# Another order of weight slices in block 0, half of a cast on ScalarE, one product on VectorE

## The chip, the cores and the metric

One core of one Trainium2 chip runs the kernel. The metric is the device time of one execution in microseconds (us), the median of several runs. The engines are named as the profile names them: PE is TensorE (matmuls; PEld its weight loads), DVE is VectorE, ACT is ScalarE, POOL is GpSimd, and SP is SyncE, which here only issues DMAs. Each engine works through its own instruction queue in order; POOL issues DMAs in the same queue in which it computes.

## The reference

Linear attention over 8 batches (B), 8 heads, 576 tokens and 64 channels, then one expert layer with an ELU over all 4608 tokens:

```python
q_s = softmax(q, axis=-1)            # over the 64 channels
k_s = softmax(k, axis=2)             # over the 576 tokens
kv  = einsum('bhsd,bhse->bhde', k_s, v)
x   = einsum('bhsd,bhde->bhse', q_s, kv)   # -> [4608, 512]
h   = x @ w_in                       # w_in  [512, 2048]
g   = where(h > 0, h, exp(min(h, 0)) - 1)
out = g @ w_out                      # w_out [2048, 512]
```

The inputs and the output are float32.

## The kernel before

The expert layer runs in nine blocks: one for 512 tokens of each batch and a last one for the 64 tokens of each batch that are left over. A block has 16 steps, one for each 128-column slice of W1 (NCH is 16). Step s of block j does, in this order: the hidden matmuls of slice s (`hidden`: four on PE into one PSUM bank, then an exponential ES on ACT and, for most slices, a subtraction on POOL), the projection of an earlier slice (`project`: four matmuls with the slice's 128 rows of W2, LAG = 3 steps behind), and the ELU's last part on DVE (`elu`, which writes GT). PE's program order is thus hidden, project, hidden, project and so on, and PE reads GT of three steps before.

While block j runs, the engines prepare batch j + 1: softmax of q (`qmax`, `qsub`, `qexp`, `qsum`, `qmul`), of k (`kmax`, `ksub`, `kexp`), v cast to bf16 (`vconv`), the product kv, its scaling (`kfac`), the transposed q (`pturn`, copied out by `pwide`), and the attention (`att`, copied out by `xc`). Batch 0 is prepared ahead of block 0, by the string START; what is woven into block 0, for batch 1, is the table FIRST. An entry of FIRST has three strings of words for a step: the first is issued after `hidden`, the second after `project`, the third after `elu`. The order in these strings is the order in which each engine gets its instructions. A word may name the engine (`:dve`, `:act`, `:gp` for POOL).

Words that matter here:

- `w1:a:b` and `w2:a:b` issue, from POOL, one DMA for slices a to b-1 of W1 or W2 (256 KB a slice). `hidden` of slice c waits for W1's slice c, `project` for W2's.
- `load:V:1:RAB` issues from SP four DMAs of 288 KB, one for each pair of heads (slots 0 to 3), into VR; the word `hold` ahead of it makes SP wait for the latest hidden matmuls. Half A of a batch means slots 0 and 1, half B slots 2 and 3.
- `vconv:A` casts half A of v into VB and waits for slots 0 and 1; `kv:A` reads it. Words for part R of v and k (`vconv:R`, `ksub:R`, `kexp:R`) issue nothing for batch 1, and `kmax2:R` nothing at all: `vconv` (L566), `ksub_slot` (L447), `kexp_slots` (L490) and `kmax` (L341) return without an instruction for that part.
- `qmul:2` and `qmul:3` are q's last products for slots 2 and 3 of batch 0, read by `pturn:B` on PE. `xc:1:dve` copies the first attention product for block 0 on DVE.
- Bank 7 (AB) of PSUM is used in turn by `kspread`, `pturn:A`, `pturn0:R`, `rest0`, `pturn:B`, `kv:A` and the attention in block 0: PE writes it, ACT copies it out, and PE may write again only then.

Of the kernel before, what the change touches and what calls it, by code (L numbers as in the profile page):

```python
# [11 lines left out]
B, H, S, D = 8, 8, 576, 64  # L12
# [3 lines left out]
R = 4  # L16
# [19 lines left out]

AT = {"rawA": 0, "rawA2": 1, "rawB": 7, "rawB2": 4, "rawS": 3, "rawT": 2,
      "kturnA": 4, "kturnB": 5, "kvA": 6, "kvB": 4, "pturnA": 5, "pturnB": 5,  # L40
      "att0": 6, "att1": 2, "att2": 3, "att3": 4, "clip": (1, 2, 4, 6, 8, 10, 11, 17, 21, 30, 32, 33, 37, 42, 44)}
START = ("load:Q:0:1 load:K:0:0 load:K:0:1 warm:1:7 warm:4:7 qmax:1 warm:2:4 load:Q:0:3 qsub:1:dve "
# [3 lines left out]
         "w1:4:6 kacross:B kexp:S vconv:A:act kmin:A qsub:2:gp qsub:3:gp diag:act:B w2:2:3 qsum:0 kmin:B "  # L46
         "kexp:A load:V:0:3 kmin:T qexp:2 qmul:A:dve qsum:2 load:V:0:2 qexp:3 w1:6:9 "
         "qsum:3 vconv:B:gp load:K:1:M qmul:2:gp kexp:B kexp:T kv:A kfac:A:dve pturn:A kv:B "
         "pwide:A:act kfac:B:act warm:1:3 att:1 att:0 qmul:3:gp pturn:B xc:1:dve xc:0 h:2:4 "
         "pwide:B:act w2:3:4 att:2 att:3 xc:2 load:Q:1:A load:Q:1:R w2:4:6 h:0:2 xc:3 kmax2:AB ")  # L50
FIRST = {
    0: ("qmax:A ksub:R:dve", "", "qsub:0:dve"),
    1: ("w1:13:14", "w1:9:12", "qsub:1:dve"),
    2: ("", "qmax0:R", "w2:6:9"),
    3: ("hold qexp:A", "load:Q:1:B:act", ""),
    4: ("w1:12:13", "w2:9:13", "load:K:1:R qsum:A qsub0:R:dve"),
    5: ("w1:14:16", "kturn", "kacross vconv:R qmax:C"),
    6: ("", "qmul:A hold", "load:V:1:RAB"),
    7: ("qexp0:R", "", "diag qsub:2:dve"),
    8: ("qsub:D", "kspread load:K:2:MR copy ksub:1 qsum0:R", "qexp:C qmulr0:dve ksub:0 qsum:C"),  # L60
    9: ("pturn:A", "", "ksub:3 kexp:R qmul:B:dve pwide:A:act"),
    10: ("", "pturn0:R pwide0:R:act", "ksub:2:dve vconv:A:gp"),
    11: ("rest0 rcopy0:act", "kexp:A", ""),
    12: ("pturn:B w2:15:16", "pwide:B:act load:Q:2:ABR", "w2:13:15"),
    13: ("kv:A vconv:B:dve", "kfac:A:dve", "kexp:B peak2:B att:0 xc:0"),
# [55 lines left out]
class Gen:  # L121
# [760 lines left out]
    def hidden(self, j, c):  # L882
# [6 lines left out]
        for x, keys in self.pieces("ES", n, NE):  # L889
            mark = ["FINE"] if n < FINE else []  # L890
            if n in AT["clip"]:
                self.op("act", lambda: a.activation(ES[:, x], ps[:, x], AF.Relu, scale=-1.0), [f"bank{bank}"], keys + mark)  # L892
# [24 lines left out]
    def elu(self, j, c):  # L917
# [4 lines left out]
        for (x, eks), (_, keys) in zip(self.pieces("ES", n, NE), self.pieces("GT", n, NG)):  # L922
            how = (ES[:, x], -1.0, ps[:, x], ALU.add, ALU.max) if n in AT["clip"] else (
                ps[:, x], 0.0, ES[:, x], ALU.max, ALU.min)
# [173 lines left out]
    def first_batch(self):  # L1098

        at = AT  # L1100
        where = {"A": (at["rawA"], at["rawA2"]), "B": (at["rawB"], at["rawB2"]),
# [3 lines left out]
                   "qsum": self.qsum, "qmul": self.qmul}  # L1105
        for word in START.split():
            name, *args = word.split(":")
# [100 lines left out]
```

## Time and profile before

| | |
|---|---|
| device time, median of 3 runs | 309.68 us (309.59 to 310.59) |
| span of the profiled execution | 308.1 us |
| its instructions | 4839 |
| granted TensorE clock | 1.000 |
| HBM read, written | 38.27 MB, 9.45 MB |

The span goes from the first to the last instruction of the one execution that was profiled; it is what the profile tells of that execution's own time. A line of the timeline reads: start and duration in us, engine, line of the kernel, operation, tile written <- tiles read, shape, number of instructions merged, and in brackets how long the engine had been idle before it and what ended that. A line of the waits reads: who waited <- for whom, us in total, times, the longest. A line of DMA issues ends with the size and the us from issue to landing. A row by windows gives, for each engine, the busy us and the number of instructions, then the granted clock, the DMA's busy share and its GB/s. The rows below are of core 0, the only one.

### The profile page before, as it was taken

The page shows a single profiled execution, that of the slowest core. Times are in us where ns is not written, and L with a number is a line of the kernel's source. Part 1 is how long each engine was busy: PE and PEld are TensorE (multiplying, and loading weights), DVE is VectorE, ACT ScalarE, POOL GpSimd, SP SyncE. Part 2 cuts the span into 40 slices and gives each one's busy share as a digit, 9 for nine tenths or more (in the row PEclk, how much of TensorE's full clock was granted, in tenths as well). Part 3 has the DMA queues.
Part 4 walks back from the last instruction along what each step waited for, and adds up shares of the span by engine and source line. Part 5 has one row for each costly group of instructions (what it writes and reads, how often), then busy time and mean ns, then how long its engine had stood idle before and what let it go on. Part 6 is the DMA issues. An engine that isn't in the chain of part 4 may idle for free.

```text
span 308.1 us, 4839 instructions
## 1 busy us (share of the span) xinstructions
PE 297.6 (97%) x1733; PEld 240.1 (78%) x1733; DVE 235.0 (76%) x400; ACT 192.9 (63%) x358; POOL 171.3 (56%) x215
## 2 busy tenths in 40 slices
PE   7789899999999999999999999999999999999995
PEld 4467677788878888888888888888888888888884
DVE  6988978979959897999889988998895353335442
ACT  2678975577559784877587758775877543334432
POOL 2968873686436743786278637863686333333440
PEclk9999999999999999999999999999999999999999
DMA  7999999985708993768475846590512030003004
GB/s 261 393 340 364 372 345 257 273 253 145 191 3 246 261 251 105 223 122 231 133 217 144 208 143 209 146 198 3 172 23 57 2 136 0 0 2 136 0 0 136
DMA packets 60584, 51.63 MB, mean 168 GB/s; under 512 B 26897, under 2 KB 50705, under 8 KB 60561
## 3 DMA queue, kind: packets, MB, share of 16 engines
q1 hardware_dynamic: 52960, 41.23, 47.7%
q0 software_dynamic: 6400, 8.39, 10.5%
q10 hardware_dynamic: 1200, 1.72, 2.0%
q8 instruction: 13, 0.21, 0.3%
q14 instruction: 11, 0.08, 0.1%
HBM read 38.27 MB, written 9.45 MB: 155 GB/s over the span
## 4 chain that ended last, share of the span: by engine, by line
PE 85%; DMA 6%; POOL 4%; ACT 2%; DVE 2%; issue 1%
PE bank L933 40%; PE bank L912 40%; DMA W2S<-in_moe_w_out_dram 5%; PE bank L827 2%; POOL W1S L255 1%; PE bank L598 1%; DMA QR<-in_q_dram 1%; POOL QR L679 1%; POOL QS L708 1%; PE bank L805 1%; DVE KT L326 1%; DVE QF L672 0%; PE bank L560 0%; ACT ES L895 0%; ACT ES L893 0%
## 5 line engine op out<-in xcount | busy, mean ns | idle before, releaser
L933 PE MATMUL bank<-W2S,GT 128*128 128x512 f32 x572 | 153.4, 391 | 1.4 <-DMA W2S<-in_moe_w_out_dram 1.2
L896 POOL TENSOR_SCALAR ES<-ES 128x512 f32<-128x512 f32 (+1 forms) x130 | 85.8, 662 | 117.3 <-ACT ES L895 117.3
L912 PE MATMUL bank<-XT,W1S 128*128 128x512 f32 x512 | 138.4, 392 | 0.5 <-issue 0.3
L925 DVE SCALAR_TENSOR_TENSOR GT<-bank,ES 128x512 fp32r<-128x512 f32 (+1 forms) x130 | 87.9, 681 | 54.4 <-PE bank L912 40.6
L933 PEld LDWEIGHTS bank<-W2S,GT 128*128 128x128 f32 x572 | 106.3, 188 | 23.6 <-DMA W2S<-in_moe_w_out_dram 1.6
L895 ACT ACTIVATE ES<-bank 128x512 f32<-128x512 f32 (+1 forms) x130 | 76.0, 592 | 70.9 <-PE bank L912 70.7
L912 PEld LDWEIGHTS bank<-XT,W1S 128*128 128x128 f32 x512 | 94.1, 188 | 19.9 <-ACT XT L814 0.9
L679 POOL TENSOR_TENSOR QR<-QR,QM 128x512 f32<-128x512 f32 (+1 forms) x21 | 24.9, 1187 | 0.6 <-DVE QM L672 0.5
L684 ACT ACTIVATE QR<-QR 128x1024 f32<-128x1024 f32 (+3 forms) x19 | 19.0, 1006 | 3.1 <-DVE QR L679 3.1
L855 ACT ACTIVATE XT<-bank 128x320 fp32r<-128x320 f32 (+1 forms) x30 | 15.0, 501 | 9.4 <-PE bank L827 9.3
L689 DVE TENSOR_REDUCE QZ<-QR 128x16 f32<-128x1024 f32 (+1 forms) x14 | 18.8, 1343 | 0.6 <-ACT QR L684 0.6
L672 DVE TENSOR_REDUCE QM<-QR 128x16 f32<-128x1024 f32 (+1 forms) x14 | 18.8, 1342 | 0.0
L912 PE MATMUL bank<-XTR,W1S 128*128 128x512 f32 x64 | 16.6, 389 | 0.0
L438 DVE TENSOR_TENSOR KR<-KR,NB 128x512 f32<-128x512 f32 x16 | 14.6, 938 | 0.0
L623 ACT ACTIVATE MB<-bank,KZ 64x64 fp32r<-64x64 f32 x44 | 10.1, 302 | 7.0 <-DVE KZ L614 6.9
L387 DVE TRANSPOSE_TENSOR_REDUCE KM<-KR 128x32 f32<-128x1024 f32 x12 | 14.4, 1226 | 0.0
L857 POOL CAST QT<-QW 128x1024 fp32r<-128x1024 f16 x12 | 12.5, 1039 | 2.9 <-DMA QW<-QS 2.9
L912 PEld LDWEIGHTS bank<-XTR,W1S 128*128 128x128 f32 x64 | 12.0, 188 | 2.5
L892 ACT ACTIVATE ES<-bank 128x512 f32<-128x512 f32 x15 | 8.9, 594 | 7.9 <-PE bank L912 7.9
L827 PE MATMUL bank<-QT,MB 128*128 128x320 f32 (+1 forms) x48 | 12.5, 300 | 0.7 <-ACT XT L855 0.7
L708 POOL TENSOR_TENSOR QS<-QR,QI 128x1024 f16<-128x1024 f32 (+1 forms) x7 | 12.5, 1783 | 0.4 <-DVE QI L691 0.4
L484 ACT ACTIVATE EK<-KR 128x1024 bf16<-128x1024 f32 x12 | 12.6, 1050 | 0.0
(108 smaller groups left out, 262.8 us busy)
## 6 DMA issues: line engine op xcount, KB each, us to landing
out_dram<-OSB SPq DMA_DIRECT2D x30, 256.0 KB, 2.7
KR<-in_k_dram SPq DMA_DIRECT2D x6, 1024.0 KB, 7.7
VR<-in_v_dram SPq DMA_DIRECT2D x6, 1024.0 KB, 6.3
QR<-in_q_dram SPq DMA_DIRECT2D x5, 1024.0 KB, 8.0
KR<-in_k_dram SPq DMA_DIRECT2D x8, 288.0 KB, 6.1
VR<-in_v_dram SPq DMA_DIRECT2D x8, 288.0 KB, 6.6
W1S<-in_moe_w_in_dram POOLq DMA_DIRECT2D x3, 768.0 KB, 9.2
QR<-in_q_dram SPq DMA_DIRECT2D x4, 512.0 KB, 11.2
```

Of the source, the lines that this page charges most:

```text
L672: self.op("dve", lambda: v.tensor_reduce(m, QR, AX.X, ALU.max), self.qkeys(b, part), self.qstat("QM", b, part))
L679: self.op(en, lambda: e.tensor_tensor(QR, QR, m, ALU.subtract), keys + self.qstat("QM", b, part), self.qown(b, part))
L684: self.op("act", lambda: a.activation(QR, QR, AF.Exp), keys, self.qown(b, part))
L689: self.op("dve", lambda: v.tensor_reduce(z, QR, AX.X, ALU.add), self.qkeys(b, part), self.qstat("QZ", b, part))
L708: self.op(en, lambda: e.tensor_tensor(out, QR, z, ALU.mult), keys + self.qstat("QI", b, part), [f"QS{x}" for x in cells])
L827: last = pe.matmul(self.bank[bank][:, a - c0:b - c0], self.MB[f][:, :, :].rearrange("p u d -> p (u d)"), self.QT[:, f, a - f * S:b - f * S ...
L855: self.op("act", lambda: e.activation(out, src, AF.Copy), reads, writes)
L895: self.op("act", lambda: a.activation(ES[:, x], ps[:, x], AF.Exp), [f"bank{bank}"], keys + mark)
L896: self.op("gp", lambda: g.tensor_scalar(ES[:, x], ES[:, x], -1.0, 1.0, ALU.add, ALU.mult), keys, keys)
L912: return pe.matmul(ps, self.W1S[:, kc, c * 128:(c + 1) * 128], x[:, kc, 0:SM], start=(kc == 0), stop=(kc == 3))
L925: self.op("dve", lambda: v.scalar_tensor_tensor(out[:, x], *how), [f"bank{bank}"] + eks + (["FINE"] if n < FINE else []), keys)
L933: return pe.matmul(self.bank[OB[t]][:, :], self.GT[n % NG][:, t * 128:(t + 1) * 128], self.W2S[:, c, :], start=(c == 0), stop=(c == NCH - ...
```

## The change

Only the strings START and FIRST are edited, and the kernel has one line less, so that every line number behind them is one lower afterwards. The diff, without the lines of START that are only wrapped anew:

```diff
 START:
-  ... kmax:2 kmax2:R load:V:0:0 ...
+  ... kmax:2 load:V:0:0 ...
-  ... pwide:A:act kfac:B:act warm:1:3 att:1 att:0 qmul:3:gp pturn:B xc:1:dve xc:0 h:2:4 ...
+  ... pwide:A:act kfac:B:act qmul:3:dve warm:1:3 att:1 att:0 pturn:B xc:1:dve xc:0 h:2:4 ...
 FIRST = {
-    0: ("qmax:A ksub:R:dve", "", "qsub:0:dve"),
-    1: ("w1:13:14", "w1:9:12", "qsub:1:dve"),
-    2: ("", "qmax0:R", "w2:6:9"),
-    3: ("hold qexp:A", "load:Q:1:B:act", ""),
-    4: ("w1:12:13", "w2:9:13", "load:K:1:R qsum:A qsub0:R:dve"),
-    5: ("w1:14:16", "kturn", "kacross vconv:R qmax:C"),
+    0: ("qmax:A", "", "qsub:0:dve"),
+    1: ("w1:9:12", "", "qsub:1:dve"),
+    2: ("qmax0:R", "", "w2:6:9"),
+    3: ("hold", "load:Q:1:B:act", ""),
+    4: ("qexp:A w1:12:14", "w2:9:11", "qsum:A qsub0:R:dve"),
+    5: ("w1:14:16", "kturn", "kacross qmax:C"),
     6: ("", "qmul:A hold", "load:V:1:RAB"),
     7: ("qexp0:R", "", "diag qsub:2:dve"),
-    8: ("qsub:D", "kspread load:K:2:MR copy ksub:1 qsum0:R", "qexp:C qmulr0:dve ksub:0 qsum:C"),
-    9: ("pturn:A", "", "ksub:3 kexp:R qmul:B:dve pwide:A:act"),
-    10: ("", "pturn0:R pwide0:R:act", "ksub:2:dve vconv:A:gp"),
+    8: ("qsub:D w2:11:13", "kspread load:K:2:MR copy ksub:1 qsum0:R", "qexp:C vconv:A:act qmulr0:dve ksub:0 qsum:C"),
+    9: ("pturn:A", "", "ksub:3 qmul:B:dve pwide:A:act"),
+    10: ("", "pturn0:R pwide0:R:act", "ksub:2:dve"),
```

What each engine's queue becomes: PE and SP keep theirs. DVE gets the product `qmul:3` (128x512) between the reciprocal KZ of half B and the copy `xc:1`. ACT gets the exponential `qexp:A` after both ES instructions of slice 4 instead of before them, and the cast `vconv:A` (128x1152) between `qexp:C` and ES of slice 9. POOL loses `qmul:3` and that cast; its DMA issues in block 0 were W1 13, W1 9 to 11, W2 6 to 8, W1 12, W2 9 to 12, W1 14 and 15, and are now W1 9 to 11, W2 6 to 8, W1 12 and 13, W2 9 and 10, W1 14 and 15, and, after `qsub:D`, W2 11 and 12.

More of the change, by code (lines that the diff above doesn't have):

```diff
@@ L33 @@
 VW = 66
[L39 to L42, printed above, removed]
[3 rows of a table removed]
[L46 to L49, printed above, removed]
+AT = {"rawA": 0, "rawA2": 1, "rawB": 7, "rawB2": 4, "rawS": 3, "rawT": 2, "kturnA": 4, "kturnB": 5,
+      "kvA": 6, "kvB": 4, "pturnA": 5, "pturnB": 5, "att0": 6, "att1": 2, "att2": 3, "att3": 4,
+      "clip": (1, 2, 4, 6, 8, 10, 11, 17, 21, 30, 32, 33, 37, 42, 44)}
@@ L50 @@
+START = ("load:Q:0:1 load:K:0:0 load:K:0:1 warm:1:7 warm:4:7 qmax:1 warm:2:4 load:Q:0:3 qsub:1:dve load:Q:0:0 "
+         "kmax:0 warm:3:5 load:K:0:2 kraw:A qexp:1 kmax:1 load:K:0:3 kturn:A load:V:0:1 qmax:0 kraw:S qsum:1 "
+         "qsub:0:gp kacross:A load:Q:0:2 kmax:3 kraw:B kmax:2 load:V:0:0 w1:1:4 w1:0:1 diag:act:A qmax:2 "
+         "kmin:S qexp:0 kraw:T kturn:B w2:0:2 qmax:3 w1:4:6 kacross:B kexp:S vconv:A:act kmin:A qsub:2:gp "
[3 rows of a table added]
          "pwide:B:act w2:3:4 att:2 att:3 xc:2 load:Q:1:A load:Q:1:R w2:4:6 h:0:2 xc:3 kmax2:AB ")
```

6 rows, old and new, of the table START are left out of this document.

## The prediction

> **What bounds the kernel now.** I read the head of the page first, then the chain that ended last.
>
> ```profile
> span 308.1 us, 4839 instructions
> PE 297.6 (97%) x1733; PEld 240.1 (78%) x1733; DVE 235.0 (76%) x400; ACT 192.9 (63%) x358; POOL 171.3 (56%) x215
> PE 85%; DMA 6%; POOL 4%; ACT 2%; DVE 2%; issue 1%
> 28.02 16.91 DMA W2S<-in_moe_w_out_dram
> ```
>
> PE is busy 97% of the span. The fourth line, from the chain in order of time, is its one long piece that is not PE: a W2 slice, issued at 28.02 us. The view of waits, asked for 34 to 46 us and then for 57 to 308 us, shows where PE can still gain:
>
> ```profile
> PE bank L933 <- DMA W2S<-in_moe_w_out_dram: 1.2, 2, 0.9
> PE bank L827 <- ACT XT L855: 0.7, 1, 0.7
> ```
>
> The first line is the earlier stretch, the second the later one. Nothing is to be won or lost after 57 us: PE waits once there, in a part that the change leaves alone. So the end moves by as much as PE's place in block 0 moves. I call cN the projection with W2 slice N (four matmuls of L933) and hN the hidden matmuls with W1 slice N (four of L912). PE in time order, c0 and then c6 to c9:
>
> ```profile
> 24.47 1.20 PE L933 MATMUL bank<-W2S,GT 128*128 128x512 f32 x4 [0.15 <-DVE GT L925]
> 37.57 1.19 PE L933 MATMUL bank<-W2S,GT 128*128 128x512 f32 x4 [0.95 <-DMA W2S<-in_moe_w_out_dram]
> 40.52 0.31 PE L766 MATMUL bank<-ID,QSR 64*64 64x64 f16 x8
> 40.76 1.20 PE L912 MATMUL bank<-XT,W1S 128*128 128x512 f32 x4
> 41.80 0.53 PE L864 MATMUL bank<-QT,MB 128*128 128x64 f32 x4
> 42.16 1.17 PE L933 MATMUL bank<-W2S,GT 128*128 128x512 f32 x4
> 43.16 1.08 PE L912 MATMUL bank<-XT,W1S 128*128 128x512 f32 x4
> 44.09 0.62 PE L744 MATMUL bank<-ID,QS 128*128 128x128 f16 x8
> 44.98 1.20 PE L933 MATMUL bank<-W2S,GT 128*128 128x512 f32 x4 [0.28 <-DMA W2S<-in_moe_w_out_dram]
> ```
>
> c6 waits 0.95 us for slices 6 to 8, c9 waits 0.28 us for slices 9 to 12. Both together, 1.23 us, are what an earlier arrival can return.
>
> **W1 and W2 in another order.** The landings, by the DMA view over each issue (the last row is the overall DMA rate in the stretch by windows):
>
> ```profile
> W1S<-in_moe_w_in_dram POOLq DMA_DIRECT2D x1, 256.0 KB, 7.9
> W2S<-in_moe_w_out_dram POOLq DMA_DIRECT2D x1, 768.0 KB, 11.8
> W2S<-in_moe_w_out_dram POOLq DMA_DIRECT2D x1, 1024.0 KB, 16.9
> 25.71 0.76 POOL L262 DMA_DIRECT2D W2S<-in_moe_w_out_dram  x1
> 24.40:36.60 12.20, 12.13 (x60) 9.79 (x60) 11.31 (x21) 10.29 (x20) 10.27 (x12) 1.00 1.40 365
> ```
>
> W2 6:9 is issued at 25.71 and lands at 37.5. Ahead of it in POOL's queue stand W1 13:14 (256 KB) and W1 9:12. The change takes the 256 KB away: 0.262 MB at 365 GB/s is 0.72 us if the DMA alone sets the pace, and its issue on POOL comes one 0.76 us issue sooner. So W2 6:9 lands at 36.8 or a little before. PE, without its wait, is there at 37.57 - 0.95 = 36.62. The first wait falls to 0.0-0.2 us; I take all 0.95 as returned. Ahead of c9 stood 256 + 768 + 768 + 256 + 1024 KB, and afterwards stand 768 + 768 + 512 + 512 KB; 512 KB less is 1.4 us at 365 GB/s, more than the 0.28. That wait goes too. W2 11:13, now issued after qsub:D, has the same bytes ahead as before and is wanted only by c11, two projections after c9. Its issue, some 0.7 us, falls into POOL's idle time for NB:
>
> ```profile
> 35.88 2.99 POOL L456 TENSOR_TENSOR KR<-KR,NB 128x576 f32<-128x576 f32 x2 [0.73 <-ACT NB L471]
> ```
>
> The edits to qmax0:R change no order on DVE, and the words for part R of batch 1 and kmax2:R issue nothing. qexp:A behind ES4 instead of ahead of it makes ES5 up to half a microsecond later; I cost it at nothing, since c5, which wants it, has c2 to c4 and h6 to h8 ahead of it on PE. The later half of batch 1's q now shares the DMA with W1 9:12 instead of W1 13:14; qexp:C wants it, and up to 1 us of lateness there is covered by ACT's wait below.
>
> **qmul:3 on DVE.** POOL loses one of two products, DVE gains one behind KZ of half B:
>
> ```profile
> 16.82 2.06 POOL L708 TENSOR_TENSOR QS<-QR,QF 128x512 f16<-128x512 f32 x2
> 17.91 0.17 DVE L614 RECIPROCAL KZ<-bank 128x2 f32<-128x2 f32 x1
> 18.48 0.69 DVE L812 CAST XT<-bank 128x512 fp32r<-128x512 f32 x1 [0.40 <-PE bank L805]
> 24.66 0.68 DVE L679 TENSOR_TENSOR QR<-QR,QM 128x512 f32<-128x512 f32 x1
> 73.26 0.95 DVE L708 TENSOR_TENSOR QS<-QR,QI 128x512 f16<-128x512 f32 x1
> 18.82 1.31 POOL L262 DMA_DIRECT2D W2S<-in_moe_w_out_dram  x2
> ```
>
> The product takes 0.68 us (like L679 at 24.66, with POOL only issuing DMAs) or 0.95 (like 73.26, beside a POOL product). POOL's remaining product ends near 17.86, before DVE starts at 18.05, so I take 0.68, of which 0.40 fills an idle gap. Starts on one engine follow each other about 0.08 us before the former ends, so the XT cast starts at 18.65 instead of 18.48: 0.17 us late (0.44 at the upper price). Behind it on DVE stand the K maxima, qmax:A and GT0, which c0 waits for: c0 and all of PE after it come 0.17 us later, 36.79 at c6. The transposes of the second half had waited for POOL's second product; they may start 0.1 us sooner, but XT on ACT holds h0 to its old time. POOL's two W2 issues come 1 us sooner, behind a queue already full.
>
> **Half of v on ScalarE.** This is the part that decides. POOL loses a cast after which it idled:
>
> ```profile
> 40.81 2.14 POOL L857 CAST VB<-VR 128x1152 bf16<-128x1152 f32 x1
> 35.73 1.27 ACT L684 ACTIVATE QR<-QR 128x1280 f32<-128x1280 f32 x1
> 36.91 0.58 ACT L895 ACTIVATE ES<-bank 128x512 f32<-128x512 f32 x1
> 37.39 1.02 ACT L788 ACTIVATE QT<-bank 128x1024 fp32r<-128x1024 f16 x1
> 39.72 0.60 ACT L892 ACTIVATE ES<-bank 128x512 f32<-128x512 f32 x1 [1.32 <-PE bank L912]
> 40.35 0.63 ACT L893 ACTIVATE ES<-ES 128x512 f32<-128x512 f32 x1
> 40.89 0.37 ACT L855 ACTIVATE QT<-bank 128x256 fp32r<-128x256 f16 x1
> 11.39 1.16 ACT L855 ACTIVATE VB<-VR 128x1152 bf16<-128x1152 f32 x1
> 30.87 0.44 SPq L277 DMA_DIRECT2D VR<-in_v_dram  x1
> VR<-in_v_dram SPq DMA_DIRECT2D x1, 288.0 KB, 7.2
> VR<-in_v_dram SPq DMA_DIRECT2D x1, 288.0 KB, 8.2
> DMA to landing us min/median/max: 5.4/6.4/9.4
> ```
>
> POOL's cast came at 40.81 and found v landed. ACT's comes right behind qexp:C, at 36.91 + 0.17 = 37.08, and needs slots 0 and 1. Slot 1 is issued at 30.87 and lands 7.2 us later, at 38.07: ACT, in order, stands still until then. Behind the wait are ES9, the QT copy of half A (L788), both steps of ES10 and the QT rest copy; PE's L766 wants bank 7 back from L788, and L864 wants the rest copy. I call T the landing of slot 1. The new cast takes 1.16, so ES9 starts at T + 1.10, L788 at T + 1.58, ES10 at T + 2.50, its second step at T + 3.13, the rest copy at T + 3.67, done at T + 4.04; L864 then starts at about T + 4.08. (L766 can start at T + 2.6, and h11 and L864 follow 1.28 later, so the rest copy is the later of the two.) From L864 PE runs 0.36 + 1.00 + 0.93 + 0.61 us to c9, by the starts quoted above less the wait of 0.28: T + 6.98. It was 44.98, so
>
> shift = T - 38.00, but not under -1.06 (the 1.23 returned less 0.17) from PE itself, and not under 37.08 - 38.00 = -0.92 from the inserted cast alone.
>
> With v's latency unchanged and its issue 0.17 us later with PE (SP waits there for h6), T is 38.24 and the shift +0.24. With the weights' queue 256 KB shorter in that stretch T may be up to 0.7 us sooner: 37.5, -0.5. I take 38.1, nearer the measured latency, as only the weights move: +0.1. Bounds: the largest latency of slots that a row shows with slot 2's 8.2 gives T = 39.24 and +1.24; the smallest, 5.4, gives -0.92; the 9.4 would give +2.4. From c9 on, kv of half A and the rest of the batch follow PE, and ACT, DVE and POOL idle there (POOL shed 2.1 us).
>
> **The sum:** 308.1 - 1.23 + 0.17 + 1.16 (the stand of ACT that PE feels, from -1.06 up to +0.1) = 308.2 us of span. The three timed runs have a median of 309.68 us, 1.58 over that span; I keep this difference: 309.8 us. About 0.3%, 0.93 us, is what a measurement of this kernel tells from no change, so that is no change.
>
> **The rivals.**
> - v comes early, before 37.08: only the inserted cast counts, 309.68 - 0.92 = 308.8. For it: fewer bytes compete. Against it: slot 1 would have to land a full microsecond sooner than it did. The Trainium skill, "DMA: Bandwidth & Descriptors", section "Queues, rings and completion order", says that each DMA engine goes round the queues that have work, packet by packet; by that rule the first two slots, 576 KB, would get half of 365 GB/s from their issue on and be there by about 34.1, an estimate. The trace disagrees with so simple a reading: 7.2 us for slot 1.
> - v comes late: the weights, pulled forward, take the DMA from v. One mechanism, at ACT's cast; it costs each microsecond in full, and decides (slower by 0.3%) from T = 38.93 on. At slot 2's latency 309.68 + 1.24 = 310.9; at 9.4 us 312.1. For it: DMA share 1.40 of the stretch, it is saturated. Against it: W2 11:13 goes out of v's way.
> - The weights do not land sooner, and c6 and c9 wait as before. PE then reaches L766 at 40.52, still before or with T + 2.6; the time stays at 309.7 to 309.9, only the profile would tell.
>
> **How the numbers follow.** The forecast (the weights' waits go, ACT's wait for v takes their place) has a chance of 0.58, with its own range of 309.2 to 310.4; v early 0.17; v late 0.21; weights unmoved 0.04. v early ends at -0.92, right at the bound, so 0.13 counts as faster with what lies beyond, 0.04 as same. Same is 0.58 + 0.04 + 0.04 = 0.66, slower 0.21. The range, 308.8 to 311.1, takes in v early and slot 2's latency.
>
> **What would show it.** Right: no DMA wait at c6 and c9; c0 at 24.64; an ACT gap of about 1 us before the v cast, ended by the landing of v; PE waits for ACT before L766 or L864, about 1 us together; from 57 us on all PE times shifted alike. Wrong: no gap on ACT (v early), a PE gap over 2 us at L766 (v late), a gap left at c6, or c0 late by 0.4 or more (product at the upper price).

## The result, and the profile after

| | before | after |
|---|---|---|
| device time, median of 8 runs each | 309.95 us (309.37 to 310.59) | 310.93 us (310.68 to 312.51) |
| ratio, with its 95% interval | | 1.0051 [1.0033, 1.0069] |
| time of the profiled execution beside its span | - / 308.1 us | 310.88 / 308.8 us |

The changed kernel is slower: by 0.98 us between the medians, and by 0.33 to 0.69% by the interval of the ratio. The forecast was 309.8 us and no change. The time lies inside the stated range of 308.8 to 311.1, but the kernel did get slower. Its eight runs fall into two groups: five from 310.68 to 310.98 at a mean granted clock of 0.999 or 1.000, and three from 312.42 to 312.51 at 0.993 to 0.995. The second group is part of the result. The changed kernel makes it itself, as the experiments show: before's 78 executions in the three later comparisons all have a clock of 0.998 or more.

From the head of the page after, its busy times, and its line of the granted clock in 40 slices:

```profile
span 308.8 us, 4839 instructions
PE 298.6 (97%) x1733; PEld 240.4 (78%) x1733; DVE 236.6 (77%) x401; ACT 194.2 (63%) x359; POOL 168.1 (54%) x213
PEclk9999999999999999999999999999999999999999
```

The profiled execution is one of the first group. Its waits from 34 to 46 us:

```profile
PE bank L765 <- ACT QT L787: 1.6, 1, 1.6
ACT VB L854 <- DMA VR<-in_v_dram: 0.9, 1, 0.9
```

PE's two waits for W2 (1.2 us in all before) are gone, and one wait of 1.6 us for ScalarE stands in their place. PE in time order, the first hidden group h0, then c0, c6, the transposition L765 and c9:

```profile
20.43 1.16 PE L911 MATMUL bank<-XT,W1S 128*128 128x512 f32 x4 [0.33 <-issue]
25.03 1.20 PE L932 MATMUL bank<-W2S,GT 128*128 128x512 f32 x4
37.01 1.17 PE L932 MATMUL bank<-W2S,GT 128*128 128x512 f32 x4
41.58 0.31 PE L765 MATMUL bank<-ID,QSR 64*64 64x64 f16 x8 [1.59 <-ACT QT L787]
45.74 1.18 PE L932 MATMUL bank<-W2S,GT 128*128 128x512 f32 x4
```

No bracket stands at c6 and c9 any more. c9 started at 44.98 before and starts at 45.74 now, and the rest follows it: from c9 to the end are 308.82 - 45.74 = 263.08 us, against 308.14 - 44.98 = 263.16 before. What holds PE up at L765 is on ScalarE: first its timeline, then the issue of v's slot 1 on SP.

```profile
36.66 1.28 ACT L683 ACTIVATE QR<-QR 128x1280 f32<-128x1280 f32 x1 [0.28 <-DVE QR L678]
38.87 1.17 ACT L854 ACTIVATE VB<-VR 128x1152 bf16<-128x1152 f32 x1 [0.93 <-DMA VR<-in_v_dram]
39.94 0.58 ACT L894 ACTIVATE ES<-bank 128x512 f32<-128x512 f32 x1
40.42 1.02 ACT L787 ACTIVATE QT<-bank 128x1024 fp32r<-128x1024 f16 x1
...
31.45 0.43 SPq L276 DMA_DIRECT2D VR<-in_v_dram  x1
```

And the DMA view of that issue:

```profile
VR<-in_v_dram SPq DMA_DIRECT2D x1, 288.0 KB, 7.3
```

Slot 1 is issued at 31.45 and lands 7.3 us later. The cast of v starts at 38.87, with 0.93 us of idle time ahead of it, and the copy L787 behind it gives bank 7 back only at 41.44.

In the same stretch there is something that the waits of PE do not name. DVE's product QSR (part R of q, which L765 transposes), and POOL at that time:

```profile
37.68 2.27 DVE L715 TENSOR_TENSOR QSR<-QR,QF 128x256 f16<-128x256 f32 x1
...
36.02 0.77 POOL L261 DMA_DIRECT2D W2S<-in_moe_w_out_dram  x1
36.82 2.83 POOL L455 TENSOR_TENSOR KR<-KR,NB 128x576 f32<-128x576 f32 x2
40.61 0.62 POOL L895 TENSOR_SCALAR ES<-ES 128x512 f32<-128x512 f32 x1 [0.96 <-ACT ES L894]
```

And the same product before:

```profile
36.75 0.83 DVE L716 TENSOR_TENSOR QSR<-QR,QF 128x256 f16<-128x256 f32 x1
```

The product takes 2.27 us instead of 0.83 and ends at 39.95, 0.3 us behind the second of POOL's two k subtractions (36.82 + 2.83 = 39.65). That is still ahead of 41.44, so here it costs nothing.

### The profile page after: what moved, and what is told of

It reads as the page before. It is cut to its first block, busy times and chain, and to the rows that moved or that the text cites. A ratio compares the mean times of both kernels' runs of the same rounds, so it can differ in the third digit from the quotient of the medians.

```text
span 308.8 us, 4839 instructions
## 1 busy us (share of the span) xinstructions
PE 298.6 (97%) x1733; PEld 240.4 (78%) x1733; DVE 236.6 (77%) x401; ACT 194.2 (63%) x359; POOL 168.1 (54%) x213
## 4 chain that ended last, share of the span: by engine, by line
PE 88%; DMA 4%; POOL 3%; DVE 2%; ACT 1%; SPq 1%; issue 1%; ACTq 0%
PE bank L932 41%; PE bank L911 40%; DMA VR<-in_v_dram 2%; PE bank L826 2%; DMA QR<-in_q_dram 2%; PE bank L597 1%; POOL W1S L254 1%; DVE KT L325 1%; POOL QR L678 1%; PE bank L559 1%; SPq L276 1%; PE bank L804 1%; POOL W2S L261 0%; ACT VB L854 0%; POOL VB L856 0%
```

## The experiments

The theory after the result: the wait of ScalarE for v costs what the weights return, and it gathers PE's idle time in one stretch long enough for the clock to drop. The rivals: the weights' new order, or the product held up on DVE, is what costs. Each diff is against the kernel named with it, cut to the words that move. Full-clock executions are those of 0.998 or more.

**1. The changed kernel again** (`after_again`, no edit).

> The changed kernel again, unedited. Its first profile had h0 0.55 us later than before, with the same instructions ahead of it on every engine. If that is the scatter of a single execution, h0 is now within 0.6 us of 19.9 either way, while h0 to c9 stays at 25.3 and h0 to the end at 288.4 us; if the changed program starts later as such, h0 is again at 20.4. On the clock: three of its eight runs had 0.993 to 0.995 and were 1.6 us longer; if the change brings that, it shows again, and not in the kernel before.

312.45 us, ratio 1.0075 [1.0048, 1.0103]: five of seven executions are at 0.992 to 0.994, the other two at 310.4. So the level of the median depends on how often the clock drops, three times in eight in the first sample and five in seven here; so few executions do not settle the share. Its profile has PE's wait of 1.56 us for ScalarE again, h0 at 20.04 and the end at 308.33: h0 to the end is 288.29 us here and 288.39 in the first profile.

**2. The weights alone** (`weights_only`, against after).

```diff
-  qmul:3:dve warm:1:3 att:1 att:0 pturn:B
+  warm:1:3 att:1 att:0 qmul:3:gp pturn:B
-  8: ... qexp:C vconv:A:act qmulr0:dve ...
+  8: ... qexp:C qmulr0:dve ...
-  10: ... ksub:2:dve
+  10: ... ksub:2:dve vconv:A:gp
```

> The changed kernel with vconv:A back on POOL in step 10 and qmul:3 back on POOL: the weights' order (and qexp:A behind ES4) alone. By the theory that ScalarE's wait for v is what eats the gain: no DMA wait at c6 and c9, no PE wait at L766, and from h0 to c9 about 25.10 - 1.23 = 23.9 us (25.10 before, 25.31 in the changed kernel); 1.0 to 1.3 us faster than before. By the rival that the weights' new order itself delays something: not faster than before, a wait left between h0 and c9.

313.56 us, the median of all twelve executions, against 310.09 for before (1.0069 [1.0029, 1.0109] for the four shortest alone). Eleven are at 0.987 to 0.995, and the one at full clock took 308.87. What the theory expected did not come: without the cast on ScalarE the kernel is not better off, and a wait is left. In the timeline, PE's row at the transposition, DVE's product, and POOL from 35 to 43 us:

```profile
42.67 0.31 PE L765 MATMUL bank<-ID,QSR 64*64 64x64 f16 x8 [3.12 <-DVE QSR L715]
...
37.31 5.31 DVE L715 TENSOR_TENSOR QSR<-QR,QF 128x256 f16<-128x256 f32 x1
...
35.66 0.78 POOL L261 DMA_DIRECT2D W2S<-in_moe_w_out_dram  x1
36.46 2.83 POOL L455 TENSOR_TENSOR KR<-KR,NB 128x576 f32<-128x576 f32 x2
39.27 0.61 POOL L895 TENSOR_SCALAR ES<-ES 128x512 f32<-128x512 f32 x1
39.86 1.39 POOL L455 TENSOR_TENSOR KR<-KR,NB 128x576 f32<-128x576 f32 x1
41.20 1.14 POOL L856 CAST VB<-VR 128x1152 bf16<-128x1152 f32 x1
```

And the granted clock from its page:

```profile
PEclk9999979999999999999999999999999999999999
```

The waits for W2 have gone from this kernel too, but POOL now works from 35.66 to 42.34 without a pause, and DVE's product of 0.5 us ends at 42.62, right behind it. PE waits 3.12 us for that product, and the sixth slice of the clock shows a 7. In the changed kernel ScalarE's wait delays ES9, so that POOL pauses for 0.96 us ahead of 40.61, and the product gets through: one loss hides another. The one execution at full clock was not profiled; its span of 307.1 us, 4.2 under this one's, leaves no room for such a wait.

**3. The product on POOL** (`weights_qsr_pool`, against weights_only).

```diff
-  8: ... qmulr0:dve ksub:0 ...
+  8: ... qmulr0:gp ksub:0 ...
```

> weights_only with one word edited: the product for q's rest (QSR, 128x256) on POOL between its two k subtractions, instead of on VectorE. In weights_only that product stood 5.31 us on VectorE (0.83 before) while POOL ran without a pause, and PE waited 3.1 us for it. If the product is held off by POOL's reads of SBUF, it is now done near 38.5 us, PE's wait at L765 and the half-clock stretch are gone, and the span is 1.0 to 1.2 us under that of before, in every run. If PE's wait has another cause (the weights' order as such), it stays above 1 us.

309.80 us, 0.9981 [0.9967, 0.9994], no execution under 0.998 and no wait at L765. It confirms that the held-up product made the 3.12 us. But the gain over before is 0.3 us and not the 1.0 to 1.2 expected, because the next product on DVE now takes 2.85 us (1.76 in before_again, 1.21 in weights_only), and PE waits for that. It ends 1.08 us behind POOL's unpaused work (at 43.38), which fits a product held up until then:

```profile
41.61 2.85 DVE L707 TENSOR_TENSOR QS<-QR,QI 128x1024 f16<-128x1024 f32 x1
...
44.52 0.62 PE L743 MATMUL bank<-ID,QS 128*128 128x128 f16 x8 [0.83 <-DVE QS L707]
```

**4. The last W2 piece issued later** (`weights_w2_later`, against weights_only).

```diff
-  8: ("qsub:D w2:11:13", ...
+  8: ("qsub:D", ...
-  9: (..., "ksub:3 qmul:B:dve pwide:A:act")
+  9: (..., "ksub:3 w2:11:13 qmul:B:dve pwide:A:act")
```

> weights_only with the issue of W2 11:13 behind POOL's third k subtraction instead of ahead of the first. POOL then stands idle for NB ahead of the first subtraction, as before the change. If that issue is what packs POOL's queue so that VectorE's QSR product is held off, the product takes 0.8 to 1.5 us again, PE's wait at L765 goes and the kernel is about 1 us faster than before. If the lateness of q's second half (VectorE's wait of 0.9 us for it) is what brings the product to the wrong place, the product still takes over 2 us and PE waits for it.

308.76 us, 0.9945 [0.9926, 0.9964]: faster than both kernels, by 1.35 us against before on the same chip (310.11). DVE, POOL, and PE's transposition and c9:

```profile
37.49 0.53 DVE L715 TENSOR_TENSOR QSR<-QR,QF 128x256 f16<-128x256 f32 x1
...
36.12 3.18 POOL L455 TENSOR_TENSOR KR<-KR,NB 128x576 f32<-128x576 f32 x2 [0.23 <-ACT NB L470]
...
39.72 0.31 PE L765 MATMUL bank<-ID,QSR 64*64 64x64 f16 x8
43.71 1.18 PE L932 MATMUL bank<-W2S,GT 128*128 128x512 f32 x4
```

The product takes 0.53 us, PE waits nowhere over 0.2 us between c0 and c9, and h0 (20.05) to c9 takes 23.66 us instead of 25.1 (24.37 in the second profile of before, experiment 11). So the new order of the weights is worth about what the forecast had put at 1.23 us (0.4%, inside the interval), provided that POOL's issue of W2 11:13 does not stand ahead of the k subtractions.

**5. The cast on ScalarE alone** (`v_act_only`, against before).

```diff
-  8: ... qexp:C qmulr0:dve ...
+  8: ... qexp:C vconv:A:act qmulr0:dve ...
-  10: ... ksub:2:dve vconv:A:gp
+  10: ... ksub:2:dve
```

> The kernel before with vconv:A on ScalarE behind qexp:C, and nothing else. If T (landing of v's slot 1) + 6.98 us sets c9, T stays near 38.1 and c9 near 45.0 to 45.2: from h0 to c9 25.1 to 25.3 us, the wait at c6 still there, no more than 0.3 us slower than before. If the cast on ScalarE costs more than this wait (its own length of 1.1 us on top), 0.8 to 1.4 us slower than before.

310.25 us, 1.0012 [0.9994, 1.0031]. ScalarE waits 1.15 us for v, PE 0.62 us for W2 at c6 and 0.58 us for ScalarE at L766; the product QSR is short (0.83), and h0 to c9 is 25.16 us, as expected. By itself the cast costs little, because PE comes late to L766 anyway.

**6. v released one hidden group earlier** (`v_early`, against after).

```diff
-  5: ("w1:14:16", "kturn", "kacross qmax:C"),
-  6: ("", "qmul:A hold", "load:V:1:RAB"),
+  5: ("w1:14:16", "kturn hold", "load:V:1:RAB kacross qmax:C"),
+  6: ("", "qmul:A", ""),
```

> The changed kernel with v's load let go one step earlier (behind h5 instead of h6), about 1.8 us sooner. By the prediction's sum alone, T + 6.98 us with T near 37, the wait for v goes and the span falls by 0.9 us or so. By the rival that VectorE's QSR product is held off by POOL: without ScalarE's wait POOL gets ES9 at once and runs without a pause until about 41.8, the product ends only then, and PE waits 1.5 us or more at L765 for VectorE instead of ScalarE: no gain.

310.34 us, 1.0012 [0.9992, 1.0033]. Neither picture was right. ScalarE no longer waits for v (the cast starts at 37.55 without idle time), but v, released at 28.56 instead of 31.06, delays W2 6:9, and PE waits for that instead. In this kernel, the DMA view of the issue of W2 6:9:

```profile
W2S<-in_moe_w_out_dram POOLq DMA_DIRECT2D x1, 768.0 KB, 13.0
```

And c6 in its timeline:

```profile
38.22 1.19 PE L932 MATMUL bank<-W2S,GT 128*128 128x512 f32 x4 [1.45 <-DMA W2S<-in_moe_w_out_dram]
```

13.0 us instead of the changed kernel's 10.7: v and the weights compete for the DMA, and the wait only changes its place. DVE's product takes 2.23 us here and ends at 39.61, 0.29 behind POOL's second k subtraction, although POOL does not pause: it goes on with ES9, which takes 0.80 us instead of 0.62. So a pause of POOL is not the only way for the product to get through.

**7. The cast late on ScalarE** (`v_act_late`, against after).

```diff
-  8: ... qexp:C vconv:A:act qmulr0:dve ...
+  8: ... qexp:C qmulr0:dve ...
-  10: ("", "pturn0:R pwide0:R:act", ...
+  10: ("", "pturn0:R pwide0:R:act vconv:A:act", ...
```

> The changed kernel with vconv:A still on ScalarE, but two steps later, behind the copy of q's rest (pwide0:R) in step 10, when v has landed. If the wait for v is the cost and not the cast's 1.16 us, PE's waits at L766 and at the W2 slices are both gone and c9 comes 23.9 to 24.3 us after h0; about 1 us faster than before. If ScalarE's own time is the cost, no faster than the changed kernel.

312.69 us, 1.0086 [1.0055, 1.0116], four of six executions at 0.988 to 0.995. It is no faster than the changed kernel, as the second picture had it, but the cause is another. ScalarE's wait for v is gone, and the held-up product comes forward: QSR takes 4.21 us and PE waits 1.85 us for it at L765. As in experiment 2, the second loss had lain behind the first.

**8. The W2 piece later in the changed kernel, and both edits together** (`after_w2_later`, with the diff of experiment 4 against after; `vlate_w2_later`, with those of 4 and 7).

> The changed kernel with the last W2 piece issued by POOL behind its k subtraction instead of ahead of its subtractions. If ScalarE's wait for v is what costs in the changed kernel, DVE's product QSR is short again (0.5 to 0.8 us instead of 2.27) and nothing else changes: TensorE still waits 1.4 to 1.7 us at the wide transposition, c9 stays within 0.3 of 25.3 behind h0, and the median is 310.5 to 312.4, with about half of the executions at a lower clock. If the held-off DVE product is what costs, TensorE's wait falls under 0.6 and the time to 309.2 or less.

> The same with the W2 piece later and, besides, ScalarE's conversion of v behind the wide transposition's copy, where v has long landed. Both waits are gone then: by the theory (the wait for v first, the held-off product behind it) TensorE has no wait over 0.5 between c0 and kv, no execution falls to a lower clock, h0 to c9 is 23.6 to 24.0, and the median is 308.7 to 309.2, about 1 us faster than before. If half a v conversion on ScalarE costs by its 1.17 us of work alone, wherever it stands, TensorE waits about 1 us somewhere behind the wide transposition, and the median is 309.8 to 310.3.

The first: 312.33 us, 1.0066 [1.0034, 1.0098], six of ten executions under 0.998. QSR is short again (0.52 us), and nothing is gained: PE waits 1.82 us for ScalarE, a little more than expected. Only c9 missed its bounds, 27.13 us behind h0, because the profiled execution is one in which the clock dropped. The second: 309.09 us, 0.9966 [0.9953, 0.9978], no execution under 0.998, h0 to c9 23.65 us. Its cast and its c9:

```profile
40.93 1.16 ACT L854 ACTIVATE VB<-VR 128x1152 bf16<-128x1152 f32 x1
...
44.20 1.18 PE L932 MATMUL bank<-W2S,GT 128*128 128x512 f32 x4
```

The same 1.16 us of work on ScalarE costs PE nothing where v has landed. The four kernels 2, 4, 7 and 8 separate the two losses: in the changed kernel the wait for v is the one that ends last, and taking it away alone brings out the other.

**9. The wait filled** (`after_filled`, against after: six unused matmuls of `warm` on PE right ahead of `pturn0:R`; nothing uses their results).

```diff
-  10: ("", "pturn0:R pwide0:R:act", ...
+  10: ("", "warm:6:1 pturn0:R pwide0:R:act", ...
+            elif name == "warm":
+                self.warm(int(args[0]), int(args[1]))
```

> The changed kernel with six more matmuls (results unused, 1.4 us) on PE right ahead of L765, where PE idles 1.6 us for ScalarE. Nothing else moves: L765 still waits for the copy of QT. If the runs of the changed kernel at a clock of 0.992 to 0.995 (8 of 15) come from that idle stretch, no run here is under 0.998 and the median falls from about 312 to 310.4 us. If the clock drop has another cause, it shows in half of the runs again.

311.01 us, 1.0025 [1.001, 1.0039]; none of its twelve executions is under 0.998. PE's timeline:

```profile
39.76 1.52 PE L1094 MATMUL bank<-GT,ONES 128*128 128x512 f32 x6
41.48 0.31 PE L765 MATMUL bank<-ID,QSR 64*64 64x64 f16 x8 [0.20 <-ACT QT L787]
```

L765 starts as late as in the changed kernel (41.48 against 41.58), only PE is busy until then. The time is about that of the changed kernel's full-clock executions (310.39 to 310.98; 310.4 had been expected), and the executions of 312.4 us are gone. So PE's idle stretch is what drops the clock.

**10. The q product back on POOL** (`q3_gp`, against after, the first pair of lines of experiment 2).

> The changed kernel with the last q product of the first batch back on POOL, where it was before. If that product on DVE is what makes the time outside the profiled span 2.0 to 2.1 us instead of 1.75 to 1.9 (as it was in every kernel with the product on DVE so far), the difference is about 1.8 here, and a full-clock execution takes 0.2 us less than the changed kernel's: 310.6. If it is chance, the difference stays at 2.05. Either way TensorE still waits about 1.6 us for ScalarE at the wide transposition, so about half of the executions lose 2 us to a lower clock: median 310.6 to 312.4.

Time less span is 1.81 us on average, as in before (1.82 over its 78 executions), against 2.04 in the changed kernel. All six kernels of this study with the product on DVE lie at 1.96 to 2.06, all six with it on POOL at 1.80 to 1.83. That the time outside the span is 0.23 us longer with the product on DVE is shown; why is not. The median is 312.79 with five of six executions under 0.998, the sixth at 310.72. Its profile is one of those five. PE's timeline at the transposition and behind it:

```profile
42.16 0.31 PE L765 MATMUL bank<-ID,QSR 64*64 64x64 f16 x8 [1.98 <-ACT QT L787]
42.40 1.91 PE L911 MATMUL bank<-XT,W1S 128*128 128x512 f32 x4
```

And the stretches by windows around the drop (columns as in the rows by windows before, the granted clock third from the end):

```profile
36.00:42.62 6.62, 4.64 (x34) 3.45 (x33) 6.39 (x9) 4.99 (x8) 5.15 (x6) 1.00 1.19 368
42.62:46.03 3.41, 3.41 (x11) 2.84 (x11) 3.24 (x4) 2.47 (x6) 0.56 (x1) 0.50 1.15 328
46.03:50.00 3.97, 3.97 (x37) 2.92 (x38) 1.44 (x3) 2.55 (x4) 1.79 (x3) 1.00 1.01 272
```

For 3.41 us, from 0.46 us after PE has started again, the clock is 0.50, with PE busy throughout. The hidden group h11, most of which lies in it, takes 1.91 us; h0 in the first profile after took 1.16. Half of 3.41 us is 1.7 us of lost work; the two groups of the changed kernel's runs lie 312.45 - 310.88 = 1.57 us apart.

**11. The kernel before, unchanged** (`before_again`).

> The kernel before, unchanged, for the scatter of one profiled execution: h0 within 19.9 to 20.7, h0 to c9 25.1 and h0 to the end 288.2 to 288.4 as in its first profile; 1.75 to 1.9 us outside the span; granted clock 0.998 or more in each execution. A shift of h0 to c9 by more than 0.3 would make the comparisons of single executions weaker than they are taken here.

309.94 us, all eight executions at 0.998 or more. h0 to c9 is not 25.1 us but 24.37, outside the bound set. The rows of h0, c6 and c9:

```profile
20.54 1.17 PE L912 MATMUL bank<-XT,W1S 128*128 128x512 f32 x4 [0.23 <-issue]
...
37.35 1.19 PE L933 MATMUL bank<-W2S,GT 128*128 128x512 f32 x4
...
44.91 1.20 PE L933 MATMUL bank<-W2S,GT 128*128 128x512 f32 x4 [0.42 <-DMA W2S<-in_moe_w_out_dram]
```

h0 is 0.66 us later than in the first profile, c9 is at the same time (44.91 against 44.98), and PE has waited 0.42 instead of 1.23 us. In the kernel before, c9 sits on the landing of W2 9:13, and a later h0 is taken out of the waits.

The clock over all kernels, by the longest wait of PE between c0 and c9 in the profiled execution:

| kernel | longest wait, us | executions under 0.998 |
|---|---|---|
| weights_w2_later, vlate_w2_later | none over 0.2 | 0 of 16 |
| after_filled | 0.20 | 0 of 12 |
| before; again | 0.95; 0.42 | 0 of 78; 0 of 8 |
| v_act_only | 0.62 | 1 of 12 |
| weights_qsr_pool | 0.83 | 0 of 12 |
| v_early | 1.45 | 2 of 12 |
| after and its repeat | 1.59, 1.56 | 8 of 15 |
| after_w2_later, v_act_late | 1.82, 1.85 | 10 of 16 |
| q3_gp | 1.98 | 5 of 6 |
| weights_only | 3.12 | 11 of 12 |

The length of the wait alone does not sort the profiles: with 1.82 us the clock dropped (after_w2_later), with 1.85 it did not (v_act_late). The traces show what does. In all fourteen the granted clock changes only at whole multiples of 3.413 us behind its first rise (in q3_gp at 5.07 + 11 x 3.413 = 42.62), and that rise lies anywhere between 4.5 and 7.9 us. Divided at these moments, the stretch that holds the wait reads, by windows, in the first profile after and in q3_gp, and the two stretches that share it in v_act_late:

```profile
38.58:41.99 3.41, 1.82 (x16) 1.23 (x15) 3.38 (x4) 3.09 (x5) 2.45 (x3) 1.00 1.21 363
39.21:42.62 3.41, 1.44 (x14) 0.93 (x13) 3.21 (x5) 3.14 (x5) 1.96 (x3) 1.00 1.20 361
37.98:41.39 3.41, 2.59 (x12) 1.79 (x10) 3.41 (x2) 2.95 (x5) 3.41 (x4) 1.00 1.19 365
41.39:44.80 3.41, 2.38 (x19) 2.07 (x20) 3.38 (x5) 2.00 (x4) 0.68 (x1) 1.00 1.16 365
```

The first figure behind the length is PE's busy time. It is 1.66 us in after_w2_later and 0.35 in weights_only. Behind these two and q3_gp's 1.44 comes a stretch at half clock; behind every other stretch from c0 to c9, with 1.82 us or more, none. So in these profiles what counts is PE's idle time within one such stretch, with a limit near half of it. The rule is read from few cases: one stretch at the end of vlate_w2_later, with 1.57 us busy, was not followed by a drop, and the one low execution of v_act_only is not explained. The changed kernel's 1.82 us is close to the limit. Its own executions at a lower clock were not profiled, but the same wait is 1.82 and 1.98 us in after_w2_later and q3_gp, where v's slot 1 took 7.6 and 7.7 us to land instead of 7.3.

## Why the prediction was wrong

**The weights' waits** go, as predicted: W2 6:9 lands at 36.26 and c6 has no wait, nor has c9. What was put at 1.23 us is the figure of one execution with an early h0, though; the second profile of before has 0.42.

**ScalarE's wait for v takes their place**, as predicted: an idle time of about 1 us ahead of the cast (0.93), ended by v's landing, a wait of PE before L765, and c9 at T + 6.98. With the measured landing, 31.45 + 7.34 = 38.79, the formula gives 45.77; c9 is at 45.74.

**The step that failed is the size of T**, "I take 38.1, nearer the measured latency": it was 38.79, 0.69 us more. The latency hardly moved (7.34 against 7.20); the issue did, from 30.87 to 31.45, because it waits for h6 and h0 stood at 20.43 instead of 19.88. That is scatter and not the change: in the second profile of the kernel before, the issue is at 31.55 and the landing at 31.55 + 7.2 = 38.8, and over the fourteen profiles of this study h0 lies between 19.88 and 20.67, with a median of 20.36, and the profile that the forecast used has the earliest. The formula set a moment that moves with h0 (T) against one that stood still in the two profiles of before (c9 on the landing of W2, at 44.98 and 44.91). With h0 at 20.36 and before's own 38.07 - 19.88 = 18.19 us from there to the landing, T is 38.55, and the hope of an earlier one, for which 0.14 us were taken off, had no support in the run. Two profiles are few, but all executions at 0.998 or more say the same: the span is 308.66 us on average in the changed kernel (7) and 308.32 before (78), 0.34 more where 0.1 had been forecast.

**The 1.58 us outside the span** was mis-sized too: it is 2.06 for the profiled execution (310.88 - 308.82). Of these 0.48 us, 0.24 come from setting a median of three runs against the span of another execution (before has 1.82 on average), which falls on both kernels alike, and 0.22 to 0.24 from the q product on DVE. Inside the span that product costs nothing, where 0.17 was forecast: h0 to c0 is 4.60 us against 4.59.

Together: 0.6 us in the span (308.8 against 308.2) and 0.48 outside it are the 1.1 us by which a full-clock execution, 310.88, lies above the forecast. The executions at a lower clock add 0.05 us to the median of this sample (310.93) and 2 us to that of the repeat (312.45 against 310.4).

**What was missing altogether is what an idle stretch does to the clock.** The sum counted PE's idle time only by its length, so that 1.23 us in two pieces, seven us apart, and 1.6 us in one seemed nearly alike. They are not: before, none of 86 executions was under 0.998; with the change, 8 of 15 were. The Trainium skill, "TensorE: Matmul & The Clock Gate", section "Part 1: The HAM clock gate (the "warmup" mystery)", says that TensorE goes to half its clock after at least one idle window of about 3.4 us, and that the window runs freely, so that the same kernel comes out differently from run to run. The half rate (0.50), the length of the window (3.41 us) and the chance in it agree with these runs; a whole idle window was not needed, since the clock also dropped after windows in which PE was busy for 1.44 and 1.66 us.

**W2 11:13** was costed at nothing, as falling "into POOL's idle time for NB". In the changed kernel that holds, because ScalarE's wait ends later. Without that wait PE waits 3.12 us (experiment 2) or 1.85 us (experiment 7) for the product on DVE; in experiment 6 the product got through in time. The Trainium skill, "SBUF — State Buffer", section "Who interferes with whom", says that a DVE instruction with two inputs in SBUF and a GpSimd instruction that reads SBUF exclude each other, and that the order of issue decides who waits. The runs agree, and show more: DVE's product was held not over one instruction but over two (the changed kernel) to five (experiment 2) in a row.

**The rivals.** "v comes late" forecast 310.9, the time that came out, but by luck, since its mechanism did not come: slot 1 took 7.34 us and not slot 2's 8.2. Experiment 6 shows the competition from the other side. "v comes early" did not happen. "The weights do not land sooner" is excluded by 36.26.

## What to carry to other kernels

Before a moment of one profile is subtracted from another, ask what each is tied to: the chain of PE, or a transfer that runs from the start; a second profile of the unchanged kernel tells it. Do not only sum PE's idle time over the kernel, but look at how much of it falls close together: here more than about 1.7 us within one of the clock's stretches of 3.41 us cost half of the next one, about as much again. And when an edit takes work out of an engine's idle time, or puts a DMA issue into it, look at what the other engine did in that pause; here two waits lay behind one another, and the weights' order gained most over before, 0.55%, with v left on POOL and W2 11:13 issued behind the subtractions.

## What the runs showed of the hardware

- In the kernels whose profiles show PE idle for 1.56 to 1.98 us in one piece, 23 of 37 executions had a mean clock under 0.998 (8 of 15, 10 of 16 and 5 of 6 in the table). In the three profiled executions that dropped, the stretch at 0.50 lasted 3.41 us, began 0.35 to 1.66 us after PE had started again, at a whole multiple of 3.413 us behind the clock's first rise, and followed a stretch in which PE was busy for 0.35 to 1.66 us. No stretch between c0 and c9 in which PE was busy for 1.82 us or more was followed by one.
- DVE's product QSR, 0.41 to 0.46 us at its shortest in other blocks, takes 0.52 to 0.84 us beside POOL's k subtractions in the six profiles in which POOL starts them after a pause, and 2.23 to 5.31 us in the seven in which a DMA issue on POOL stands right ahead of them. In six of the seven it ends about 0.3 us behind POOL's unpaused work, in v_early while POOL goes on. Why the issue decides who goes first was not tried.
- A product of 0.69 us on DVE ahead of block 0 instead of on POOL adds 0.23 us outside the profiled span, and nothing that shows inside (h0 to c0 4.60 us against 4.59).
